# Distance table made on GpSimd from index patterns, first transfers reordered, 64-row products padded to 128 rows

## Chip, cores and metric

The kernel runs on one core of a Trainium2 chip. The metric is the device time of one execution in microseconds (us). Engines are named as the profile names them: PE (matrix products; PEld is its weight load), DVE (vector), ACT (scalar), POOL (GpSimd), and SP, whose queue starts nearly all transfers (SPq).

## The reference

Attention over 2 batches x 8 heads, 768 tokens, head size 64, followed by a low-rank token mixing with an FFN, and by a Fourier mixing with a normalisation and a second FFN. Cut to what matters:

```python
scores = q @ k.T / 8                               # per head
rel = pos[:, None] - pos[None, :]
is_global = pos[None, :] < n_global                # 8
is_local = (rel >= 0) & (rel < n_local)            # 96
dist = where(is_global & ~is_local, n_local, abs(rel))
scores = where(is_global | is_local, scores - slope[h] * dist, -1e9)
x = softmax(scores) @ v                            # -> (2, 768, 512)
u = x + (x.T @ U @ V).T                            # U (768, 32), V (32, 768)
x = u + relu(u @ w1) @ w2                          # w1 (512, 2048)
u = x + real(fft(fft(x, axis=1), axis=2))
x = u + relu(norm(u) @ w1b) @ w2b
```

All inputs are float32.

## The kernel before, in words

The program is written with a tile framework: `setup` is traced first, then `arm`, inside a branch on a flag that the device computes from the two window sizes (L70 to L72, L853). Python generators (`attn`, `lr`, `ffn`, `fft`, `norm`) yield after small steps; `arm` and `drive` interleave them. From this trace the framework's planner chooses each engine's fixed order: what is traced earlier has priority, but an instruction whose inputs are ready in the planner's own clock may be put ahead of an earlier one that still waits. Every engine, and the SP queue, then works strictly in its order. Nothing inside the branch is mixed with what is outside it.

**Start.** `setup` makes a 128 x 128 identity on POOL (a memset and one affine select, listed as masks.py), and starts on the SP queue: the window sizes `n` (L48), the table `rel` (L51), query and windowed keys of head pair 0 in two halves of 64 partitions each (L55), and the values of pair 0 (`v_load`, L408). `rel` (128 x 1184 float32: eight blocks of 128 columns with -4 x distance, or -4 x 2^20 where nothing is to be kept, and two key index patterns) is laid into the second value buffer `vb[1]`. `attn_setup` (L369) turns it with the window sizes into the mask-and-distance tables `dist[0]` (DVE, L375 to L381) and `dist[1]` (POOL, L382, half of the first). 16 products of the identity with itself (`warm`, L80) stand on PE before the branch, 10 behind it, and two after each of the first six steps of attention.

**Attention.** `attn` (L413) works on 8 head pairs c, each in three units j. A unit's steps: s1 (scores L448 and L451 on PE with 64 rows for each head, then L456 on DVE adds the table), s2 (exponential on ACT, L468), s3 (transposes on PE, L479, copied out by ACT L481 or DVE L483), s5 (weights times values, L499). s1 of unit 0 of pair c starts the loads of query and keys of pair c+1 (`qk_load`, L398 and L399); s5 of unit 2 starts the values of pair c+2. Pair 1's values go to `vb[1]`, so `v_load(1)` waits until `rel` has been read.

**Low rank.** `lr_load` (L276) loads U and V (four copies of V, L283); `lr_setup` and `lr_setup2` decode them (they come as 8-byte words; L163 on ACT, L165, L167, L169 on DVE) and split them into a high and a low float32r part: `vh` (128 rows, L311) and `vl` (64 rows, L312, on POOL). `lr` (L339) then adds, for each of 6 token tiles of a batch, two products into one bank: L352 (`vh`, 128 rows) and L353 (`vl`, 64 rows, with the first 64 rows of R).

**FFN.** `ffn` (L185) runs 96 chunks: 12 products L202, then 12 products L224, all 128 x 128 weights times 512 columns in float32r (high times high, high times low, low times high). The weights of a chunk are loaded, split by ACT (L178) and POOL (L181), and in layer 1's first pass also decoded and written back.

**Fourier mixing.** `fft` (L613, once per batch) is four groups of products beside the FFN. Each accumulation ends in one product with 64 rows, which carries the one odd row of a fold: L674 (`alt` with `em`, twice per batch), L684 (the same for one odd column; its 64 weight columns are one column repeated by `spread`, as are those of the nine L682 before it), L709 (`pr` with `sgn`, four times per batch; the fourth time with a single weight column). `fft_open` loads the constant tables on POOL's queue (L604, L608).

## Time and profile before

| | us |
|---|---|
| median of 3 runs | 728.35 |
| lowest, highest | 726.04, 732.85 |
| the profiled execution | 723.43 |
| its span, first to last instruction | 721.4 |

PE was busy for 700.0 us of the span (97%), DVE for 347.2, ACT for 294.9, POOL for 299.9; the mean granted TensorE clock was 0.996 of full speed. Times below are us from the start of the span. A busy PE is not PE at its peak: products overlap, so what a product costs is read from the start of one to the start of the next.

### The profile page before, as it was taken

Reading aid. Unit: us, or ns where it says so; the run is one execution under the profiler, and the core shown is the slowest. Engines: PE = TensorE matmul, PEld = TensorE weight load, DVE = VectorE, ACT = ScalarE, POOL = GpSimd, SP = SyncE. Lnnn points to the kernel's source line nnn. Section 1 sums busy time; section 2 is a strip of 40 time slices with the busy share of each in tenths; the row PEclk is TensorE's granted clock in tenths of the full one; section 3 lists DMA queues with packets and bytes.
Section 4 is the critical chain, followed back from the end, with each engine's and each line's share of the span. In section 5 each row is a group of like instructions: output and inputs, shape, how many; then the busy total and the mean of one; then the engine's idle time right before and its main releaser. Section 6 shows DMA issues by size and latency. Waiting matters only on the chain.

```text
span 721.4 us, 9681 instructions
## 1 busy us (share of the span) xinstructions
PE 700.0 (97%) x3584; PEld 561.7 (78%) x3584; DVE 347.2 (48%) x703; ACT 294.9 (41%) x551; POOL 299.9 (42%) x256
## 2 busy tenths in 40 slices
PE   8899999989899999999999999999999999999996
PEld 7666667767678888888788878888888888888885
DVE  3898887544652744348545769113733111211112
ACT  3877755644433434344343334322333333233230
POOL 1211202316646444556424564433554445445441
PEclk9999999999999999999999999999999999999999
DMA  8785648454658467775754442212124222242211
GB/s 274 245 322 190 223 165 254 141 174 135 216 171 255 154 228 254 247 259 178 261 176 146 146 175 89 87 59 88 58 88 159 100 93 88 99 164 87 91 56 64
DMA packets 34393, 116.54 MB, mean 162 GB/s; under 512 B 4128, under 2 KB 4384, under 8 KB 32032
## 3 DMA queue, kind: packets, MB, share of 16 engines
q1 hardware_dynamic: 33024, 112.24, 46.2%
q0 software_dynamic: 1312, 3.59, 1.6%
q8 instruction: 30, 0.49, 0.3%
q14 instruction: 27, 0.22, 0.1%
HBM read 95.88 MB, written 19.92 MB: 161 GB/s over the span
## 4 chain that ended last, share of the span: by engine, by line
PE 72%; DMA 8%; DVE 6%; POOL 5%; issue 5%; ACT 3%; SPq 0%; ACTq 0%; DVEq 0%; POOLq 0%
PE ps_acc L224 29%; PE ps_h L202 29%; DMA wr<-wl 6%; POOL wo L181 5%; PE ps_sd L499 3%; PE ps_h L479 2%; PE ps_acc L448 2%; DMA lrt<-U 1%; DVE w L169 1%; PE ps_sd L267 1%; ACT wh L178 1%; DMA w<-wscr 1%; DVE xl L334 1%; ACT wr L163 1%; PE ps_sd L448 1%
## 5 line engine op out<-in xcount | busy, mean ns | idle before, releaser
L181 POOL TENSOR_TENSOR wo<-w,wh 128x512 fp32r<-128x512 f32 x192 | 256.0, 1354 | 306.3 <-ACT wh L178 304.7
L202 PE MATMUL ps_h<-uT,wh 128*128 128x512 f32 x768 | 240.8, 394 | 0.0
L202 PEld LDWEIGHTS ps_h<-uT,wh 128*128 128x128 f32 x768 | 141.3, 188 | 30.0 <-issue 2.8
L178 ACT CAST wh<-w 128x1024 fp32r<-128x1024 f32 x96 | 100.9, 1051 | 153.5 <-PE ps_acc L224 137.3
L210 DVE SCALAR_TENSOR_TENSOR gl<-ps_h,gh 128x512 fp32r<-128x512 f32 x96 | 65.9, 687 | 188.7 <-ACT gh L209 188.6
L224 PE MATMUL ps_acc<-wh,gh 128*128 128x512 f32 x384 | 152.9, 398 | 0.0
L224 PE MATMUL ps_acc<-wh,gl 128*128 128x512 f32 x384 | 150.3, 391 | 0.8 <-DVE gl L210 0.8
L202 PE MATMUL ps_h<-uT,wo 128*128 128x512 f32 x384 | 150.1, 391 | 0.0
L224 PE MATMUL ps_acc<-wo,gh 128*128 128x512 f32 x384 | 149.7, 390 | 0.0
L209 ACT ACTIVATE gh<-ps_h 128x512 fp32r<-128x512 f32 x96 | 57.2, 596 | 123.3 <-PE ps_h L202 123.0
L224 PEld LDWEIGHTS ps_acc<-wh,gl 128*128 128x128 f32 x384 | 72.1, 188 | 17.3 <-DVE gl L210 1.9
L224 PEld LDWEIGHTS ps_acc<-wh,gh 128*128 128x128 f32 x384 | 72.1, 188 | 16.5 <-issue 2.0
L202 PEld LDWEIGHTS ps_h<-uT,wo 128*128 128x128 f32 x384 | 72.3, 188 | 15.7 <-issue 0.2
L224 PEld LDWEIGHTS ps_acc<-wo,gh 128*128 128x128 f32 x384 | 72.2, 188 | 13.8
L163 ACT ACTIVATE wr<-wr 128x1024 f32<-128x1024 f32 x32 | 37.4, 1168 | 62.8 <-DMA wr<-wl 58.9
L468 ACT ACTIVATE T<-T,m 128x256 f32<-128x256 f32 (+1 forms) x96 | 47.7, 498 | 32.4 <-DVE m L456 31.2
L165 DVE TENSOR_SCALAR wr<-wr 128x1024 int32<-128x1024 int32 x32 | 24.8, 780 | 41.0 <-DMA wr<-wl 40.9
L169 DVE SCALAR_TENSOR_TENSOR wd<-wr 128x1024 int32<-128x1024 int32 x16 | 19.6, 1224 | 48.0 <-POOL wo L181 42.9
L167 DVE SCALAR_TENSOR_TENSOR wr<-wr 128x1024 int32<-128x1024 int32 x32 | 40.4, 1264 | 4.3 <-ACT wr L163 4.1
L499 PE MATMUL ps_sd<-pt,vb 128*64 128x128 f32 x384 | 34.8, 288 | 3.4 <-ACT pt L481 3.3
L499 PEld LDWEIGHTS ps_sd<-pt,vb 128*64 128x64 f32 x384 | 26.0, 139 | 11.1 <-issue 5.3
L456 DVE CUSTOM_DVE_ANT_0 T<-ps_acc,dist 128x256 f32<-128x256 f32 (+1 forms) x76 | 28.0, 419 | 5.6 <-PE ps_acc L451 3.6
(160 smaller groups left out, 606.0 us busy)
## 6 DMA issues: line engine op xcount, KB each, us to landing
w<-wscr SPq DMA_DIRECT2D x80, 512.0 KB, 3.3
wr<-wl SPq DMA_DIRECT2D x17, 1024.0 KB, 6.0
wr<-wl SPq DMA_DIRECT2D x60, 256.0 KB, 4.5
wscr<-w SPq DMA_DIRECT2D x16, 512.0 KB, 6.7
wscr<-wd SPq DMA_DIRECT2D x16, 512.0 KB, 2.9
vb<-vw SPq DMA_DIRECT2D x8, 768.0 KB, 5.4
out<-qkt SPq DMA_DIRECT2D x12, 256.0 KB, 3.3
k<-qkg SPq DMA_DIRECT2D x4, 704.0 KB, 8.5
```

The lines of the kernel that those rows point to most:

```text
L163: nc.scalar.activation(hi.bitcast(F32), hi.bitcast(F32), AF.Copy, scale=2.0 ** -112)
L167: nc.vector.scalar_tensor_tensor(lo, hi, 3, lo, ALU.logical_shift_left, ALU.bitwise_or)
L169: nc.vector.scalar_tensor_tensor(out.bitcast(I32), hi, -2147483648, lo, ALU.bitwise_and, ALU.bitwise_or)
L178: nc.scalar.copy(hi, raw)
L181: nc.gpsimd.tensor_tensor(lo[:, h], raw[:, h], hi[:, h].bitcast(F32), ALU.subtract)
L202: nc.tensor.matmul(hp, lhsT=w[:, s], rhs=u[:, dd, :], start=n == 0, stop=n == 11)
L209: nc.scalar.activation(gh, hp, AF.Relu)
L210: nc.vector.scalar_tensor_tensor(gl, hp, 0.0, gh.bitcast(F32), ALU.max, ALU.subtract)
L224: nc.tensor.matmul(acc[t], lhsT=g[:, s], rhs=w[:, D:2 * D], start=pf == 0 and m == 0, stop=pf == NF - 1 and m == 2)
L456: nc.vector.tensor_tensor_reduce(out=T[z][:, s], in0=sp[z][:, s], in1=self.dist[z][:, dcol[t]:dcol[t] + width[t]], op0=ALU.add, op1=ALU.mi ...
L468: nc.scalar.activation(T[z][:, s], T[z][:, s], AF.Exp, bias=m[z][:, i:i + 1], scale=-1.0, accum_out=st["s", c, z][:, j, i:i + 1])
L499: nc.tensor.matmul(pv[y * HD:(y + 1) * HD, z * P:(z + 1) * P], lhsT=v[:, vc, d], rhs=pt[z][:, o:o + P], start=i == 0, stop=i == n - 1)
```

## The change

The load of `rel` is gone; `rel_make` writes the same 1184 columns with 15 POOL instructions (seven iotas for the blocks and keys, two affine selects, three memsets, then an iota, a select and a memset for the last 256 columns). `v_load(1)` moves from ahead of attention to behind its second step, `lr_load` from behind the sixth step to behind the twelfth; `lr_setup` still comes after 22. The 64-row operands `vl`, `alt`, `sgn`, `em` get 64 more rows of zeros (one memset each, on POOL for `vl`, else on DVE), `pr` and the two column-spread products get 128 weight columns in place of 64 or 1, so that L353, L674, L684, L709 become 128-row products and L682, L684 and the fourth L707 and L709 have 128 columns.

```diff
--- before.py
+++ after.py
@@ -48,12 +48,12 @@
         nc.sync.dma_start(ni.rearrange("p a b -> p (a b)"), self.rows(a["n"].bitcast(I32), 4))
         self.qk, self.v = {}, {}
         self.rel, self.key = self.vb[1][:, 0:WTAB], self.vb[1][:, WTAB:WTAB + P + 32]
-        nc.sync.dma_start(self.vb[1][:, 0:WTAB + P + 32], a["rel"])
         self.qk = {0: (self.qkt[:, 0:S], self.qkt[:, S:S + KW])}
         for z in range(2):
             s = slice(z * HD, (z + 1) * HD)
             nc.sync.dma_start(self.qkt[s, 0:S + KW], a["qkg"][0][s])
         self.v_load(0)
+        self.rel_make()
         ok = cp.tile([1, 4], F32, name="ok")
         nc.scalar.activation(ok[:, 3:4], self.ident[0:1, 0:1], AF.Exp)
         nf = cp.tile([P, 2, 2], F32, name="nf")
@@ -293,7 +293,8 @@
         uraw = ur.rearrange("p (t r) -> p t r", t=NT)
         self.us = pool.tile([P, NT, 4 * RK], FR, name="us")
         self.vh = pool.tile([P, S], FR, name="vh")
-        self.vl = pool.tile([2 * RK, S], FR, name="vl")
+        self.vl = pool.tile([P, S], FR, name="vl")
+        nc.gpsimd.memset(self.vl[2 * RK:P, :].bitcast(F32), 0.0)
         us = self.us
         for c in (0, 2):
             h, l = us[:, :, c * RK:(c + 1) * RK], us[:, :, (c + 1) * RK:(c + 2) * RK]
@@ -309,7 +310,7 @@
             self.decode(vraw, v64, z)
             yield
         nc.scalar.copy(self.vh, vraw)
-        nc.gpsimd.tensor_tensor(self.vl, vraw[0:2 * RK, :], self.vh[0:2 * RK, :].bitcast(F32), ALU.subtract)
+        nc.gpsimd.tensor_tensor(self.vl[0:2 * RK, :], vraw[0:2 * RK, :], self.vh[0:2 * RK, :].bitcast(F32), ALU.subtract)
         yield
 
     def w_first(self):
@@ -350,7 +351,7 @@
             s = slice(t * P, (t + 1) * P)
             hp = self.psum("m")
             nc.tensor.matmul(hp, lhsT=self.vh[:, s], rhs=R, start=True, stop=False)
-            nc.tensor.matmul(hp, lhsT=self.vl[:, s], rhs=R[0:64, :], start=False, stop=True)
+            nc.tensor.matmul(hp, lhsT=self.vl[:, s], rhs=R, start=False, stop=True)
             nc.vector.tensor_tensor(x, hp, x, ALU.add)
             yield
             if t > 0 and b * NT + t - 1 in tiles:
@@ -365,6 +366,38 @@
             self.transpose_in(layer, i, srcs[i])
             yield
 
+
+
+    def rel_make(self):
+        g = self.nc.gpsimd
+        FAR = -4.0 * (1 << 20)
+
+        def put(out, base, step, ch, blocks=None):
+            pat = [[4, P]] if blocks is None else [[step, blocks], [4, P]]
+            v = out if blocks is None else out.rearrange("p (a c) -> p a c", a=blocks)
+            g.iota(v, pat, base=base, channel_multiplier=ch, allow_small_or_imprecise_dtypes=True)
+
+        def cut(o, base, ch, blocks=1):
+            v = self.rel[:, o:o + blocks * P].rearrange("p (a c) -> p a c", a=blocks)
+            g.affine_select(out=v, in_=v, compare_op=ALU.is_ge, fill=FAR, base=base,
+                            pattern=[[0, blocks], [-1, P]], channel_multiplier=ch)
+
+        rel = self.rel
+        put(rel[:, 384:640], -512, -512, 4, 2)
+        put(rel[:, 0:256], 0, 0, -4, 2)
+        cut(384, P, -1)
+        cut(0, 0, 1, 2)
+        put(rel[:, 256:384], -512, 0, -4)
+        put(rel[:, 640:768], -4 * 511, 0, 4)
+        put(rel[0:1, 640:768], -4 * 127, 0, 0)
+        g.memset(rel[0:1, 384:640], FAR)
+        for o in (256, 512):
+            g.memset(rel[:, o:o + 32], FAR)
+        g.iota(self.key[:, 0:P], [[1, P]], base=0, channel_multiplier=0, allow_small_or_imprecise_dtypes=True)
+        g.iota(self.key[:, P:P + 32], [[1, 32]], base=0, channel_multiplier=0, allow_small_or_imprecise_dtypes=True)
+        put(rel[:, 768:1024], -4 * 127, -512, 4, 2)
+        cut(768, P - 1, -1)
+        g.memset(rel[:, 896:928], FAR)
 
     def attn_setup(self):
         nc = self.nc
@@ -604,8 +637,9 @@
                 nc.gpsimd.dma_start(t, a[f"{n}{z}"])
                 self.ct[n, z] = t
         for n, r, w in (("alt", 64, J1), ("sgn", 64, K1)):
-            t = fp.tile([r, w], FR, name=n)
-            nc.gpsimd.dma_start(t, a[n])
+            t = fp.tile([P, w], FR, name=n)
+            nc.vector.memset(t[r:P, :].bitcast(F32), 0.0)
+            nc.gpsimd.dma_start(t[0:r, :], a[n])
             self.ct[n] = t
         self.mh = fp.tile([P, 1], F32, name="mh")
         nc.vector.memset(self.mh, -0.5)
@@ -648,18 +682,19 @@
             fold(P, E, False, ee[0][:, i, :], ee[1][:, i, :], i)
             fold(P, O, True, oo[0][:, i, :], oo[1][:, i, :], i)
             yield
-        em = fp.tile([64, K1], FR, tag="em", bufs=1, name=f"em{b}")
-        fold(64, xm, False, em, None, 0)
+        em = fp.tile([P, K1], FR, tag="em", bufs=1, name=f"em{b}")
+        nc.vector.memset(em[64:P, :].bitcast(F32), 0.0)
+        fold(64, xm, False, em[0:64, :], None, 0)
         yield
         c1, s1, c2, s2 = ([ct[n, 0], ct[n, 1]] for n in ("c1", "s1", "c2", "s2"))
         pt = fp.tile([P, 2, 2, J1], FR, tag="fpt", bufs=1, name=f"fpt{b}")
         qt = fp.tile([P, 2, 2, 384], FR, tag="fqt", bufs=1, name=f"fqt{b}")
         pt, qt = [pt[:, z] for z in range(2)], [qt[:, z] for z in range(2)]
-        pr = fp.tile([64, J1], FR, tag="fpr", bufs=1, name=f"fpr{b}")
+        pr = fp.tile([P, J1], FR, tag="fpr", bufs=1, name=f"fpr{b}")
         PS = ((0, 0), (0, 1), (1, 0))
 
         def spread(col):
-            return bass.AP(col.tensor, col.offset, [list(col.ap[0]), [0, 64]])
+            return bass.AP(col.tensor, col.offset, [list(col.ap[0]), [0, P]])
 
         for dd in range(2):
             cs = slice(dd * P, dd * P + P)
@@ -675,7 +710,7 @@
             nc.scalar.copy(pt[0][:, dd, :], pp)
             nc.vector.tensor_tensor(pt[1][:, dd, :], pp, pt[0][:, dd, :].bitcast(F32), ALU.subtract)
             yield
-        pp = self.psum("m")[0:64, 0:J1]
+        pp = self.psum("m")[:, 0:J1]
         n = 0
         for i in range(3):
             for x, y in PS:
@@ -702,11 +737,12 @@
 
         def pcos(out, js):
             n = 0
+            at = (lambda v: spread(v[:, 384:385])) if js is None else (lambda v: v[:, js])
             for dd in range(2):
                 for x, y in PS:
-                    nc.tensor.matmul(out, lhsT=pt[x][:, dd, js], rhs=c2[y][:, dd, :], start=n == 0, stop=False)
+                    nc.tensor.matmul(out, lhsT=at(pt[x][:, dd, :]), rhs=c2[y][:, dd, :], start=n == 0, stop=False)
                     n += 1
-            nc.tensor.matmul(out, lhsT=pr[:, js], rhs=ct["sgn"], start=False, stop=True)
+            nc.tensor.matmul(out, lhsT=at(pr), rhs=ct["sgn"], start=False, stop=True)
 
         for i in range(3):
             js = slice(i * P, (i + 1) * P)
@@ -730,7 +766,7 @@
                 nc.vector.tensor_tensor(X[:, 511:256:-1], X[:, 511:256:-1], hi_[:, 1:256], ALU.add)
             yield
         pc = self.psum("m")
-        pcos(pc[0:1, 0:K1], slice(384, 385))
+        pcos(pc[:, 0:K1], None)
         X = Bp[0]
         nc.vector.tensor_tensor(X[0:1, 0:257], pc[0:1, 0:257], xm[0:1, 0:257], ALU.add)
         nc.vector.tensor_tensor(X[0:1, 511:256:-1], pc[0:1, 1:256], xm[0:1, 511:256:-1], ALU.add)
@@ -786,14 +822,16 @@
         pg.at = pool
         pg.side_mode = False
         if fast:
-            pg.v_load(1)
             att = pg.attn(pool)
             pg.warm(10)
-            for _ in range(6):
+            for z in range(6):
                 step(att, 1)
+                if z == 1:
+                    pg.v_load(1)
                 pg.warm(2)
+            step(att, 6)
             pg.lr_load()
-            step(att, 16)
+            step(att, 10)
             for _ in pg.lr_setup(pool):
                 step(att, 2)
             pg.w_load(0)
```

## Rows read from the trace of the kernel before

**Rows 1.** Stretches: length, busy PE, PEld, DVE, ACT, POOL; clock, DMA share, GB/s.
```profile
86.00:99.00 13.00, 12.85 (x89) 8.50 (x84) 11.42 (x30) 7.82 (x23) 0.00 (x0) 1.00 0.74 251
194.00:520.00 326.00, 325.25 (x1483) 264.14 (x1484) 169.41 (x271) 117.29 (x163) 156.88 (x131) 1.00 0.51 172
```
**Rows 2.** Waits of PE from 194 to 520: total, times, longest.
```profile
PE ps_acc L224 <- DVE gl L210: 0.8, 2, 0.5
```
**Rows 3.** Chain that ended last, pieces: start, length, what.
```profile
10.38 8.95 DMA lrt<-U
...
92.54 0.43 PE ps_acc L353
...
217.71 2.72 PE ps_h L202 x12
```
**Rows 4.** Timeline of PE around one low-rank pair: start, length, what.
```profile
204.44 0.40 PE L352 MATMUL ps_sd<-R,vh 128*128 128x512 f32 x1
204.76 0.49 PE L353 MATMUL ps_sd<-R,vl 64*128 64x512 f32 x1
205.19 0.73 PE L202 MATMUL ps_h<-uT,wh 128*128 128x512 f32 x2
205.75 0.40 PE L202 MATMUL ps_h<-uT,wo 128*128 128x512 f32 x1
```
**Rows 5.** Groups by form, 64-row products: count, busy, mean ns.
```profile
L353 PE MATMUL ps_sd<-R,vl 64*128 64x512 f32 x6 | 3.0, 494 | 0.0
L709 PE MATMUL ps_sd<-sgn,fpr 64*128 64x258 f32 x6 | 2.3, 381 | 0.0
L674 PE MATMUL ps_sd<-alt,em 64*128 64x386 f32 x4 | 1.8, 443 | 0.0
L709 PE MATMUL ps_sd<-sgn,fpr 64*1 64x258 f32 x2 | 0.5, 272 | 0.0
```
**Rows 6.** Timeline of PE before and after the wide spread products.
```profile
359.02 0.39 PE L224 MATMUL ps_acc<-wh,gl 128*128 128x512 f32 x1
359.24 1.75 PE L682 MATMUL ps_sd<-c,ee 128*64 128x386 f32 x9
```
**Rows 7.** Timeline of DVE at the start.
```profile
5.91 0.30 DVE L375 TENSOR_SCALAR vb<-vb,nv 128x160 f32<-128x160 f32 x1 [0.97 <-DMA vb<-rel]
8.12 0.83 DVE L381 SCALAR_TENSOR_TENSOR dist<-vb,nv,dist 128x128 f32<-128x128 f32 x4
11.91 0.29 DVE L456 CUSTOM_DVE_ANT_0 T<-ps_acc,dist 128x128 f32<-128x128 f32 x1 [2.85 <-PE ps_acc L451]
19.35 0.26 DVE L165 TENSOR_SCALAR lrt<-lrt 128x192 int32<-128x192 int32 x1 [3.64 <-DMA lrt<-U]
```
**Rows 8.** Timeline of PE at the start.
```profile
10.91 0.70 PE L448 MATMUL ps_acc<-qkt 64*128 64x128 f32 x5 [1.18 <-DMA qkt<-qkg]
20.35 0.85 PE L479 MATMUL ps_h<-ident,T 128*128 128x128 f32 x6 [2.03 <-DVE pt L483]
```
**Rows 9.** Timeline of the SP queue: start, length, transfer.
```profile
17.75 0.35 SPq L398 DMA_DIRECT2D qkt<-qkg  x1
18.62 0.42 SPq L129 DMA_DIRECT2D wr<-wl  x1
29.18 0.33 SPq L408 DMA_DIRECT2D vb<-vw  x1
```
**Rows 10.** DMA issues: count, KB each, us from issue to landing.
```profile
vb<-rel SPq DMA_DIRECT2D x1, 592.0 KB, 4.7
```
**Rows 11.** Stretches of the start, columns as in rows 1.
```profile
5.00:9.00 4.00, 4.00 (x36) 4.00 (x36) 3.05 (x9) 0.00 (x0) 0.00 (x0) 1.00 1.06 243
11.00:17.00 6.00, 6.00 (x50) 5.18 (x52) 2.93 (x16) 4.40 (x17) 0.83 (x1) 1.00 1.03 411
```
**Rows 12.** Timeline of POOL at the start.
```profile
1.01 0.29 POOL masks.py:199 TENSOR_SCALAR_AFFINE_SELECT ident<-ident 128x128 f32<-128x128 f32 x1
```
**Rows 13.** The page's costliest group, on POOL: busy, mean ns | idle before, releaser.
```profile
L181 POOL TENSOR_TENSOR wo<-w,wh 128x512 fp32r<-128x512 f32 x192 | 256.0, 1354 | 306.3 <-ACT wh L178 304.7
```

## Prediction

> **What bounds the kernel now.** I read the busy times by stretch first, then the waits of PE, then the chain that ended last, and the timelines of the start last. From 194 to 520 PE is busy for 325.25 of 326 us while no other engine reaches 170 [rows 1], and in all that time its longest kind of wait, for DVE, adds up to 0.8 us [rows 2]; behind 520 nothing changes in the code. So there a product that goes, or gets cheaper, shortens the run one for one. Before 194 the stages differ. At the very start PE and DVE wait for transfers: DVE stands 3.64 us in front of the decoding of U, which lands at 19.35, though that decoding has no hurry; it only stands early in DVE's order, and the copy of the first transposes behind it holds PE for 2.03 us [rows 7, 8]. The chain confirms it: its earliest long piece is U's transfer, 10.38 to 19.33 [rows 3]. Between, around 86 to 99, PE is busy nearly throughout, but its products there are short, and DVE with 11.42 of 13 us is near its limit too [rows 1].
>
> **The padded products.** There are 22 products with 64 rows: twelve L353, four L674, two L684, six L709 with 128 columns and two with one (the rows show six of the L353; the others and the L684 follow from the code) [rows 5]. Their cost isn't their own length alone. The normal step is 2.72 us for 12 products of 512 columns, 0.227 us each [rows 3]. Around one pair the starts are 204.44 (L352), 204.76 (L353), 205.19 and, two products on, 205.75 [rows 4]: four products of 512 columns in 1.31 us in place of 0.91, so 0.40 us too much. It stands in three places: about 0.09 before the 64-row product may start, 0.20 on itself, 0.11 on what follows. With 128 rows, nothing but the normal step should stay. Outside the first six L353 there are 16 products of full width (6 + 4 + 6) at 0.40, 6.4 us; the narrow L709 is 109 ns shorter than the wide one [rows 5], so I price the two of it and the two L684 at 0.29, 1.2 us. All 20 lie between 194 and 520: 7.5 us (7.6 rounded down, since 258 columns may lose a little less). From below I would only believe the modelled lengths, which show some 0.1 us too much for each (494 ns [rows 5] against 0.40 us of a normal one [rows 4]): 2.0 us. From above 20 x 0.40, 8.0 us.
>
> The first six L353 lie among products of attention that themselves use 64 rows, so that the change of form moves rather than goes. The chain does run through them, 0.43 us each [rows 3]. Fully saved they are worth 6 x 0.40 = 2.4, hidden 0; I take 1.0, because DVE is nearly full there.
>
> The Trainium skill, "TensorEngine Tiling (Array Packing)", section Key Properties, says that a change of tiling mode drains TensorE. It lists column widths among the modes; by that the change from 128 to 64 weight columns and back in the nine L682 would cost as well, and widening them would give back, by an estimate, 0.2 us twice over in each batch, making the padding 8.3. The trace agrees for rows and differs for columns: L224 at 359.02 is followed by the first L682 at 359.24, the normal step [rows 6]. The rows decide: nothing for columns.
>
> **The first transfers.** `rel` is 592 KB, 0.606 MB. It takes 4.7 us from issue to landing [rows 10], most of it latency. The transfer engines are full from 5 us on, at 243 GB/s while the 64-partition halves of the query load and at 411 GB/s later [rows 11]; 0.606 MB is 1.5 us at the one rate and 2.5 at the other. Everything queued behind it comes that much earlier; I take 2.0 us. U now stands behind pair 1's query, keys and values, as before, so it lands at about 17.3. Is the wait on U still last? The first scores could start 1.18 us earlier, where PE now waits for the second half of the query [rows 8], so the first DVE step comes at 10.7 and DVE is free for U at 14.5, still ahead of 17.3. What follows on PE is then 2.0 us earlier. If U's decoding moves back in DVE's order, the wait goes altogether, and the limit is PE's own: 2.03 and 1.18 of idle time, 3.2 us. Behind the start the shift should pass to the end: pair 1's data are 2 us earlier too, later loads are released by PE.
>
> **The table on POOL.** The first twelve instructions of `rel_make` make the 768 columns and the keys, 1,760 columns written in all; the last three are beside DVE's first part. No iota is in the trace. The nearest row is an affine select of 128 columns, 0.29 us, 2.3 ns a column [rows 12]; by it, 4.0 us, ready at 1.3 + 4.0 = 5.3, earlier than the 5.91 at which DVE now starts on `rel` [rows 7]. From above, the dearest kind of POOL row, 1.354 us [rows 13], twelve times is 16.2 us, ready at 17.5. DVE then needs 3.1 us (5.91 to 8.95), and from the first score step to the copy behind U 3.8 (11.91 to 19.35 less the wait of 3.64) [rows 7]. The copy starts at 19.5 now; with the table ready at 12.6 it would start there without any wait for U. So the table costs nothing up to 10.4 (where U at 17.3 is still last), and at 17.5 it is 4.9 us late against now. I take 0, by the nearest row.
>
> **What is added elsewhere.** `v_load(1)` now has two loads ahead of it and still waits until the table is read, at about 8.5; `lr_load` stands behind it on the SP queue and waits with it, but what is ahead in the transfer queue keeps that busy until 12 or so: nothing. The memset of `vl` (64 x 768) goes to POOL, which waits 306 us in total for ACT [rows 13]; the memsets of `alt`, `sgn` and twice `em`, about 0.4 us each by an estimate from the 0.30 us of 160 columns [rows 7], go to DVE, busy for 169 of 326 us [rows 1]. Where DVE is late for PE now (0.8 us [rows 2]) they may add a little: 0.3 us. Without that cover all of it would cost 1.6.
>
> **The sum.** 7.5 + 1.0 + 2.0 - 0.3 = 10.2 us. The profiled execution took 723.43 us (span 721.4 and 2.0 around it), so it would take 713.2. That execution is 4.9 us below the median of the runs shown, 728.35; taken from that, 718.2 us.
>
> **Rivals.** (a) *U falls behind pair 2.* `lr_load` is now traced behind the step that asks for pair 2's query and keys. If the planner keeps that order, those wait for PE (17.75 now [rows 9], 16.5 then), and U, with 1.1 MB ahead of it, lands at about 21.5; with its decoding where it stands, the start loses 2.2 us in place of gaining 2.0: gain 6.0, 722.4 us. Against it: a weight load that is traced later already goes ahead of the values that wait for PE (18.62 before 29.18 [rows 9]), so what is ready isn't kept back.
> (b) *The rows don't matter.* The extra step belongs to something else, such as a bank or the operands' place: padding gains nothing, 2.0 - 0.3, 726.7 us. Against it: the step is the same for four lines with different operands. The Trainium skill speaks for it: "TensorE: Matmul & The Clock Gate", section Why this matters for your kernels, has a product with few rows take as long as one with 128. The trace disagrees, 0.43 us against 0.23 [rows 4].
> (c) *Slower: the table comes late.* Each iota may cost far more than a select, or each change between the two kinds may stop POOL. The start loses from a table ready at 12.6, and the whole change loses once it loses 8.2 there, with the table ready at 20.8: twelve instructions in 19.5 us, 1.6 us each, more than the dearest row. At 22 us of POOL the table is ready at 23.3, the copy starts at 30.2, 10.7 us late, and the time is 728.35 + 10.7 - 8.2 = 730.9. For it: no row shows an iota. Against it: the select follows its memset without a gap [rows 12]. The Trainium skill, "GPSIMD Engine Reference", section Instruction dispatch, tells of about 6 us, unseen in the profile, for the first call of a newly loaded kernel; three such loads would give just these 22 us, one would still hide behind U. No run here shows one.
>
> **How the numbers follow.** Forecast 0.70, (a) 0.16, (b) 0.07, (c) 0.07. The likeliest case alone runs from 8.0 + 2.4 + 3.2 = 13.6 gained to 7.5 + 1.5 - 0.5 = 8.5, so 714.7 to 719.9. The runs of before lie 2.3 below and 4.5 above their median; with that and (a) the range is 712 to 726. A change of 1% (7.3 us) is about what a measurement tells from none. Faster by more: 0.63 of the forecast's 0.70, 0.06 of (a): 0.69. Slower by more: part of (c), with a table later still: 0.03. The rest, 0.28, is within 1%.
>
> **What would show it.** Starts around L353, L674 and L709 at the normal step (0.23, 0.17, 0.12 us), their sum some 7 to 8 us; U's landing at 17 to 17.5 and the transposes behind it at about 18.3 in place of 20.35; `rel_make` finished before 6; and the point where PE becomes saturated 3 us earlier. The prediction is wrong if iotas take over a microsecond each, if U lands after 19.3, or if the steps of the padded products stay at 0.3 us or more; also if a different planned order in attention or the first FFN block, which nothing in the trace of before can show, gives back what the start gained.

## The result, and the profile after

The changed kernel takes 718.77 us (median of 6 runs, 715.34 to 720.31) against 727.25 us (6 runs, 724.39 to 732.85): ratio 0.9889, 95% interval 0.9856 to 0.9923. Forecast were 718.2 us and a range of 712 to 726. The total came as forecast; its make-up did not, and most of what follows is about that.

One caution for every comparison of traces below. The profiled execution of before (723.43 us) lies 3.8 us under the median of its runs and below all six of them; that of the changed kernel (720.31) is the slowest of its six. So the two traces differ by 3.1 us only, where the medians differ by 8.5. Their spans hide another microsecond: the last chunk starts 3.9 us earlier than before, but from the start of PE's last product to the end it took 6.17 us in the trace of before and 7.19 in that of after. I therefore follow the starts of the FFN's chunks.

The page's busy times (share of the span, instructions), against 700.0, 347.2, 294.9 and 299.9 us before:

```profile
PE 692.2 (96%) x3584; PEld 563.0 (78%) x3584; DVE 346.9 (48%) x707; ACT 294.3 (41%) x551; POOL 301.3 (42%) x272
```

**The start.** The timeline of the changed kernel on POOL, SP, DVE and PE (SPq is SP's issue of a transfer; brackets give the engine's idle time before the row, and what ended it); it answers to [rows 7 to 9, 12].

```profile
0.98 0.35 POOL L378 IOTA vb<- 128x256 f32 x1
1.30 0.28 POOL masks.py:199 TENSOR_SCALAR_AFFINE_SELECT ident<-ident 128x128 f32<-128x128 f32 x1
...
4.16 0.29 POOL L382 TENSOR_SCALAR_AFFINE_SELECT vb<-vb 128x128 f32<-128x128 f32 x1
4.39 0.12 POOL L400 MEMSET vb<- 128x32 f32 x1
...
4.74 0.60 DVE L410 TENSOR_SCALAR dist<-vb,nv 128x768 f32<-128x768 f32 x1
...
7.97 0.33 SPq L441 DMA_DIRECT2D vb<-vw  x1
8.40 0.38 SPq L280 DMA_DIRECT2D lrt<-U  x1
...
11.13 0.29 DVE L489 CUSTOM_DVE_ANT_0 T<-ps_acc,dist 128x128 f32<-128x128 f32 x1 [2.67 <-PE ps_acc L484]
...
16.14 0.26 DVE L165 TENSOR_SCALAR lrt<-lrt 128x192 int32<-128x192 int32 x1 [1.40 <-DMA lrt<-U]
...
17.20 1.04 PE L512 MATMUL ps_h<-ident,T 128*128 128x128 f32 x8
```

An iota of 256 columns takes 0.34 us and the whole of `rel_make` is over at 4.51; DVE begins on the table at 4.74 without a wait, directly behind its own set-up. U lands at 16.14 instead of 19.35, DVE waits 1.40 us for it instead of 3.64, and the second transposes start at 17.20 instead of 20.35. U's transfer starts at 8.40, ahead of pair 2's query at 16.79, so rival (a) of the prediction did not come.

**The padded products.** The groups by form and one low-rank pair in the timeline, changed kernel, in answer to [rows 4, 5].

```profile
L354 PE MATMUL ps_sd<-R,vl 128*128 128x512 f32 x6 | 2.4, 393 | 0.0
L745 PE MATMUL ps_sd<-sgn,fpr 128*128 128x258 f32 x8 | 2.2, 281 | 0.0
L709 PE MATMUL ps_sd<-alt,em 128*128 128x386 f32 x4 | 1.4, 338 | 0.0
```
```profile
199.85 0.40 PE L202 MATMUL ps_h<-uT,wo 128*128 128x512 f32 x1
200.09 0.40 PE L353 MATMUL ps_sd<-R,vh 128*128 128x512 f32 x1
200.32 0.39 PE L354 MATMUL ps_sd<-R,vl 128*128 128x512 f32 x1
200.55 0.62 PE L202 MATMUL ps_h<-uT,wh 128*128 128x512 f32 x2
```

From start to start it is now 0.23 us before, on and behind the padded product, where [rows 4] showed 0.32 and 0.43, and 0.56 for the next two together (0.46 is normal). The Fourier products' steps are normal too in this trace: 0.18 us around L709 and L719, 0.12 around L745.

**And yet PE waits.** PE's waits of the changed kernel from 194 to 520 (line, releaser: us in total, times, longest) and the two stretches of [rows 1], with two short ones. Columns of the second fence: length, busy PE, PEld, DVE, ACT, POOL, granted clock, DMA share, GB/s.

```profile
PE ps_acc L224 <- DVE gl L210: 2.4, 3, 1.0
PE ps_h L202 <- POOL wo L181: 1.6, 1, 1.6
PE ps_acc L224 <- ACT gh L209: 1.2, 1, 1.2
PE ps_sd L353 <- DVE xall L355: 0.5, 1, 0.5
```
```profile
86.00:99.00 13.00, 12.69 (x77) 8.44 (x77) 11.54 (x29) 7.57 (x21) 0.83 (x1) 1.00 0.79 257
194.00:520.00 326.00, 320.10 (x1482) 266.15 (x1482) 171.27 (x276) 117.77 (x164) 156.90 (x133) 0.99 0.50 168
...
213.00:218.00 5.00, 3.08 (x13) 1.95 (x12) 3.49 (x5) 3.08 (x4) 0.91 (x1) 1.00 1.02 376
218.00:222.00 4.00, 4.00 (x13) 3.10 (x12) 0.23 (x1) 0.24 (x1) 4.00 (x7) 0.57 0.42 140
```

The PE that stood still for 0.75 us of these 326 now does so for 5.9. From 213 to 218 it is busy for 3.08 of 5 us, and behind these gaps the granted clock has a mean of 0.57 from 218 to 222: for a time it was at the lower of its two levels, 1.2 GHz.

**Where the time went.** First product of a chunk against the kernel before, us (negative is earlier), worked out from the traces' starts of L202; "unit 3" is the first score product of pair 1. The last column is the last chunk.

```
kernel          unit 3   c0    c10    c12    c14    c34    c36    c44    c46    c52   last
before at        22.81 104.86 194.79 211.53 222.99 333.92 347.40 405.93 418.48 453.34
changed          -3.18  -7.27  -4.63  -5.56  -1.52  -1.44  -0.95  -3.29  -1.30  -1.30  -3.90
after_again      -3.16  -6.93  -5.28  -5.37  -0.99   0.27   0.75  -1.56  -0.25  -0.27  -2.87
pad_only         -0.52  -1.56  -1.06  -1.71   0.92   1.86   2.40   0.09   1.40   1.38  -1.23
start_only       -2.80  -6.11  -4.50  -3.90  -3.90  -2.96  -2.19  -2.19  -1.59  -1.62  -1.62
fft_pad_only            -6.51  -4.09  -3.54  -3.52  -3.68  -3.19  -4.88  -2.79  -2.85  -5.45
cols_narrow             -6.56  -4.52  -6.05  -3.25  -3.45  -3.16  -5.47  -3.79  -3.79  -6.39
wr16_pool               -7.54  -5.86  -7.34  -5.00  -5.18  -5.15  -7.47  -5.77  -5.80  -8.40
wr17_pool        -2.96  -7.36  -5.68  -7.42  -7.42  -6.88  -6.40  -8.71  -7.22  -7.25  -9.85
xm_dve                  -7.21  -5.38  -6.02  -3.34  -3.42  -2.94  -5.05  -3.28  -3.30  -5.90
both_supplies           -6.33  -4.11  -5.18  -5.18  -4.79  -4.31  -6.36  -5.49  -5.52  -8.12
old_loads        -2.54  -3.60  -3.50  -3.87  -1.65  -1.08  -0.61  -2.67  -0.89  -0.92  -3.52
table_x3          0.29  -3.96  -2.62  -3.82   0.22   0.97   1.44  -0.87   0.96   0.90  -1.71
u_first_w4       -3.20  -3.73  -3.21  -4.95  -0.94   0.13   0.62  -1.59   0.52   0.50  -2.10
```

In the changed kernel's line, the Fourier padding shows at c36 to c44 (2.34 us) and from c52 on (2.60). In *start_only*, which has no padding, both stretches gain nothing. Three places give time back: c0 to c10 (2.6), c12 to c14 (4.0), and c44 to c46 (2.0). The experiments ask what these are.

### The profile page after: what moved, and what is told of

It reads as the page before. It is cut to its first block, busy times and chain, and to the rows that moved or that the text cites. A ratio compares the mean times of both kernels' runs of the same rounds, so it can differ in the third digit from the quotient of the medians.

```text
span 718.5 us, 9700 instructions
## 1 busy us (share of the span) xinstructions
PE 692.2 (96%) x3584; PEld 563.0 (78%) x3584; DVE 346.9 (48%) x707; ACT 294.3 (41%) x551; POOL 301.3 (42%) x272
## 4 chain that ended last, share of the span: by engine, by line
PE 73%; DVE 7%; DMA 7%; POOL 5%; issue 4%; ACT 3%; SPq 0%; ACTq 0%; POOLq 0%; DVEq 0%
PE ps_acc L224 30%; PE ps_h L202 29%; DMA wr<-wl 7%; POOL wo L181 4%; PE ps_sd L532 2%; PE ps_acc L481 2%; PE wu L80 2%; PE ps_h L512 1%; ACT T L501 1%; PE ps_sd L267 1%; ACT wh L178 1%; PE ps_sd L729 1%; DVE w L169 1%; POOL xl L335 1%; PE ps_sd L705 1%
## 5 line engine op out<-in xcount | busy, mean ns | idle before, releaser
L181 POOL TENSOR_TENSOR wo<-w,wh 128x512 fp32r<-128x512 f32 x192 | 254.2, 1345 | 313.9 <-ACT wh L178 312.3
L202 PE MATMUL ps_h<-uT,wh 128*128 128x512 f32 x768 | 241.2, 395 | 0.0
L202 PEld LDWEIGHTS ps_h<-uT,wh 128*128 128x128 f32 x768 | 142.3, 189 | 29.6 <-issue 2.0
L224 PE MATMUL ps_acc<-wh,gl 128*128 128x512 f32 x384 | 151.1, 394 | 2.4 <-DVE gl L210 2.4
L224 PE MATMUL ps_acc<-wh,gh 128*128 128x512 f32 x384 | 152.2, 396 | 1.2 <-ACT gh L209 1.2
L202 PE MATMUL ps_h<-uT,wo 128*128 128x512 f32 x384 | 150.8, 393 | 1.6 <-POOL wo L181 1.6
L224 PE MATMUL ps_acc<-wo,gh 128*128 128x512 f32 x384 | 150.5, 392 | 0.0
L224 PEld LDWEIGHTS ps_acc<-wh,gl 128*128 128x128 f32 x384 | 72.5, 189 | 19.1 <-DVE gl L210 3.6
L202 PEld LDWEIGHTS ps_h<-uT,wo 128*128 128x128 f32 x384 | 72.4, 189 | 17.5 <-POOL wo L181 2.0
L224 PEld LDWEIGHTS ps_acc<-wh,gh 128*128 128x128 f32 x384 | 72.5, 189 | 16.4 <-ACT gh L209 1.7
L224 PEld LDWEIGHTS ps_acc<-wo,gh 128*128 128x128 f32 x384 | 72.5, 189 | 13.8
L532 PE MATMUL ps_sd<-pt,vb 128*64 128x128 f32 x384 | 32.5, 282 | 4.2 <-ACT pt L514 4.1
```

The lines of the kernel that those rows point to most:

```text
L181: nc.gpsimd.tensor_tensor(lo[:, h], raw[:, h], hi[:, h].bitcast(F32), ALU.subtract)
L202: nc.tensor.matmul(hp, lhsT=w[:, s], rhs=u[:, dd, :], start=n == 0, stop=n == 11)
L224: nc.tensor.matmul(acc[t], lhsT=g[:, s], rhs=w[:, D:2 * D], start=pf == 0 and m == 0, stop=pf == NF - 1 and m == 2)
L532: nc.tensor.matmul(pv[y * HD:(y + 1) * HD, z * P:(z + 1) * P], lhsT=v[:, vc, d], rhs=pt[z][:, o:o + P], start=i == 0, stop=i == n - 1)
```

## The experiments

**Each half alone, and the whole again.** *pad_only* has the padding alone, the table and the loads as before; *start_only* has the table and the moved loads alone. The main lines of *start_only*'s edit against before:

```diff
-        nc.sync.dma_start(self.vb[1][:, 0:WTAB + P + 32], a["rel"])
+        self.rel_make()
...
-            pg.v_load(1)
...
+                if z == 1:
+                    pg.v_load(1)
```

*after_again* is the changed kernel unaltered, for a second profile; *cols_narrow* is the changed kernel with the weights of L717 and L719 narrowed to 64 columns again, and of the last pass of L743 and L745 to one (the 64 rows of `pr` that are then not written are zeroed on DVE, not shown):

```diff
-            return bass.AP(col.tensor, col.offset, [list(col.ap[0]), [0, P]])
+            return bass.AP(col.tensor, col.offset, [list(col.ap[0]), [0, 64]])
```

> The kernel before with the padding alone: rel is loaded again, v_load(1) and lr_load stand where they stood. Theory (the padding carries most of the gain, product by product): the steps around the 20 padded products between 194 and 520 fall by 0.3 to 0.4 us each, 7.5 us in all, U lands at 19.3 as before, and the time falls by 7 to 8.5 us, a ratio of 0.988 to 0.991. Rival 1 (the start carries it, the padded steps are given back at other waits): a fall of under 4 us, ratio above 0.9945. Rival 2 (a planned order that only by chance is better): the starts of the first FFN chunk come 3 us or more earlier although nothing of the start has changed.

> The kernel before with the table on POOL and the moved loads, 64-row products as before. Theory: U lands 3.2 us earlier as in the changed kernel, PE's transposes of unit 1 start at 17.2 in place of 20.35, and 2 to 3.5 us of it reach the end: ratio 0.995 to 0.9975. Rival 1 (the start carries the gain): 5 us or more, ratio below 0.993. Rival 2 (the start's gain is given back to the weight loads between 130 and 220): under 1 us, ratio above 0.9985, with first FFN products that start 3 us or more earlier.

> The changed kernel, unaltered, for a second profile. The first one showed PE losing about 4 us between 214 and 222 (waits on ACT and DVE behind a weight load that landed late, and 3.4 us at half the granted clock). If that belongs to the order of the program, it stands here again in the same chunk (13 of the FFN), and the clock falls there again; if it belongs to that one execution, the shift of the FFN's starts against the kernel before stays between 4 and 7 us over chunks 12 to 16, and the span is 3 to 5 us below 718.5.

> The changed kernel with its 128 rows, but the spread products with 64 weight columns and the last cosine product with one, as before. If only the rows matter: each step around L682, L684 and the fourth L707 and L709 stays at 0.17 to 0.18 (386 columns) and 0.12 us (258 columns), and the time is that of the changed kernel within 1 us. If a change of column width drains PE as well: about 0.1 us before and 0.1 to 0.2 us behind each of the four groups, 0.8 to 1.2 us in all.

Measured, against 725.64 us for before: *pad_only* 724.51, ratio 0.9978 (0.9952 to 1.0004); *start_only* 722.74, 0.9956 (0.9932 to 0.9981); *after_again* 719.35, 0.9911 (0.9877 to 0.9945); *cols_narrow* 718.10, 0.9901 (0.9875 to 0.9927).

*start_only* came in its range. *pad_only* missed by far: each step fell as argued, but the time fell by 1.1 us, as its rival 1 had it, and its interval reaches past 1. Its line in the table says where: 2.6 us lost from c12 to c14, 1.3 from c44 to c46. *after_again* loses at the same places, so the losses belong to the program and not to one execution. *cols_narrow* cannot be told from the changed kernel. Its timeline on PE has the narrow products in normal steps, 0.23 us from L224 to the first of them (355.38, 355.61) and 0.18 each:

```profile
355.38 0.39 PE L224 MATMUL ps_acc<-wh,gl 128*128 128x512 f32 x1
355.61 1.75 PE L718 MATMUL ps_sd<-c,ee 128*64 128x386 f32 x9
357.19 0.34 PE L720 MATMUL ps_sd<-alt,em 128*64 128x386 f32 x1
357.37 0.39 PE L224 MATMUL ps_acc<-wh,gh 128*128 128x512 f32 x1
```

The last cosine product with one weight column has its normal 0.12 us too. So it is the rows alone, as the prediction had it against the Trainium skill ("TensorEngine Tiling (Array Packing)", section Key Properties): that page has a change of tiling mode drain the engine, and counts column widths among the modes.

**What stands at c12 to c14.** The changed kernel there, on SP, POOL, ACT and PE:

```profile
203.42 2.20 SPq L129 DMA_DIRECT2D wr<-wl  x4
...
204.71 1.33 POOL L637 DMA_DIRECT2D c<-c  x2 [3.01 <-PE ps_sd L354]
...
209.48 1.10 POOL L637 DMA_DIRECT2D s<-s  x2
210.56 0.55 POOL L637 DMA_DIRECT2D c<-c  x1
...
214.42 1.17 ACT L163 ACTIVATE wr<-wr 128x1024 f32<-128x1024 f32 x1 [5.76 <-DMA wr<-wl]
215.49 0.58 ACT L209 ACTIVATE gh<-ps_h 128x512 fp32r<-128x512 f32 x1
...
216.12 0.50 PE L224 MATMUL ps_acc<-wh,gh 128*128 128x512 f32 x1 [1.24 <-ACT gh L209]
217.54 0.50 PE L224 MATMUL ps_acc<-wh,gl 128*128 128x512 f32 x1 [0.68 <-DVE gl L210]
```

A weight load in four parts is issued at 203.42; from 204.71 the Fourier constants come on POOL's queue, released by the last low-rank product (L354). The load is there only at 214.4. ACT stands 5.76 us in front of its decoding, and `gh`, for which PE waits, stands behind that in ACT's order (it is chunk 12's, which PE uses behind chunk 13's L202). Two edits test it: take the competing transfers away from the load, or leave the low-rank products as long as they were, so that PE asks later and releases the constants later. At first I moved the wrong load, the one ahead of it (k is NF for *wr16_pool*, NF + 1 for *wr17_pool*; the four parts are NF + 1). *fft_pad_only* leaves the low-rank products at 64 rows.

```diff
-        self.nc.sync.dma_start(self.wraw[k].rearrange("p n t -> p (n t)")[:, s],
+        (self.nc.gpsimd if k == NF + 1 else self.nc.sync).dma_start(self.wraw[k].rearrange("p n t -> p (n t)")[:, s],
```
```diff
-        self.vl = pool.tile([P, S], FR, name="vl")
-        nc.gpsimd.memset(self.vl[2 * RK:P, :].bitcast(F32), 0.0)
+        self.vl = pool.tile([2 * RK, S], FR, name="vl")
...
-            nc.tensor.matmul(hp, lhsT=self.vl[:, s], rhs=R, start=False, stop=True)
+            nc.tensor.matmul(hp, lhsT=self.vl[:, s], rhs=R[0:64, :], start=False, stop=True)
```

> The changed kernel, but the load of layer 1's first weights (wr16, 1 MB) goes on POOL's queue, directly ahead of the Fourier constants (3.6 MB), instead of on SP's queue beside them. Theory (supply): in the changed kernel this load takes about 11 us (issued 203.4 to 205.2, landing 214.4) because it shares the transfer engines with the constants; ACT's decode of it stands ahead of chunk 13's gh, so PE waits 1.4 + 0.85 us and falls to half clock for 3.4 us. With the load first in one queue it lands within 6 us of its issue, ACT does not wait, PE has no wait over 0.5 us between 200 and 225 and no half clock there; chunk 14 starts 4.0 to 5.5 us earlier than in the kernel before (changed kernel: 1.5 and 1.0), and the time is 2.5 to 4 us below the changed kernel: 715 to 717. Rival (the two queues are not what makes it late; the weights' own chain does): chunk 14 stays 1 to 2 us earlier than before, time 718 to 720.

> The changed kernel with the twelve low-rank products L354 left at 64 rows; the Fourier ones stay padded. Theory (supply): what padding saves in the second six (2.4 us) only brings PE earlier to a wait for weights at chunk 13, so giving it back costs less than it: chunk 14 starts no more than 0.5 us later than in the changed kernel, perhaps earlier if PE then misses the wait and the half clock, and the time is within 1.5 us of the changed kernel, 717.5 to 720.5. Rival (each padded product pays one for one, as predicted): 2.4 us for the second six and 1.0 for the first, time 3.4 us above the changed kernel, 721.5 to 723.

> The changed kernel, but layer 1's second weights (wr17, 1 MB in four parts, the load that was issued 203.4 to 205.2 and landed at 214.4) go on POOL's queue directly ahead of the Fourier constants. The run wr16_pool had moved the load before it, and there the four parts still took 11 us. Theory (supply): alone at the head of the one queue the four parts land within 7 us of the first issue; the decode on ACT no longer holds gh of chunk 13, so both PE waits at 213 to 217 (1.4 and 0.85 us) and the half clock behind them are gone; chunk 14 starts 4.5 to 5.5 us earlier than in the kernel before and the time is 714.5 to 717. Rival (PE is ahead of something else there too, for instance gl or the weights read back): other waits of 1.5 us or more in all stand between 205 and 222, chunk 14 is 1 to 3 us earlier than before, time 717.5 to 720.

*wr16_pool*: 717.04 us, ratio 0.985 (0.9796 to 0.9904). Its time is at the upper end of the range (717), but not for the reason given: the four parts still landed at 212.5, 10.8 us after their issue, and PE still waited for `gh`; what is missing is half clock behind it. *fft_pad_only*: 718.60, 0.9858 (0.9800 to 0.9917), the same as the changed kernel, and c14 comes 2.0 us earlier than there although six products are 0.40 us dearer each. *wr17_pool*: 715.35 (714.62 to 716.83), 0.9840 (0.9805 to 0.9876). Its timeline on POOL and ACT:

```profile
201.46 2.41 POOL L129 DMA_DIRECT2D wr<-wl  x4 [1.57 <-DVE w L169]
203.85 0.56 POOL L637 DMA_DIRECT2D c<-c  x1
...
208.24 1.18 ACT L163 ACTIVATE wr<-wr 128x1024 f32<-128x1024 f32 x1 [2.69 <-DMA wr<-wl]
209.28 0.61 ACT L269 CAST uT<-ps_sd 128x512 fp32r<-128x512 f32 x1
209.75 0.64 ACT L209 ACTIVATE gh<-ps_h 128x512 fp32r<-128x512 f32 x1
```
```profile
213.00:218.00 5.00, 5.00 (x24) 4.14 (x23) 0.69 (x1) 1.65 (x2) 4.73 (x7) 1.00 1.08 367
218.00:222.00 4.00, 4.00 (x19) 3.30 (x19) 0.69 (x1) 1.35 (x2) 1.49 (x2) 1.00 1.16 326
```

The load is there 6.8 us after its issue, PE has no wait and full clock (second fence, the stretches as above), and from c12 to c14 nothing is lost. The time is in its range; c14 comes 7.42 us earlier than before, where 4.5 to 5.5 were expected. The shift at the last chunk is 9.85 us instead of 3.90, of which 1.9 us were there by c12, ahead of this load. (The planner also put the decoding one copy earlier in ACT's order.) So the stall is shown to be the late load; the edit took away the constants beside it and the SP queue together.

What made the load late can be read by setting all the traces side by side. The columns, worked out from the starts, count us from the issue of the load's first part: to the first constant's issue, to ACT's decoding, to `gh` of chunk 12 being done, and to the moment PE could use it (the last L202 of chunk 13 and one normal step); the last is what is lost from c12 to c14. The nine kernels of the second line are the changed one, *after_again*, *pad_only*, *cols_narrow*, *wr16_pool*, *xm_dve*, *old_loads*, *table_x3* and *u_first_w4*.

```
kernel                             constants   decoding      gh done     PE asks    lost
before, start_only, fft_pad_only   1.88-1.89   8.0-8.8       9.6-10.4    12.1       0.0
nine with low-rank padding         1.25-1.32   10.7-11.3     12.4-13.0   11.2-11.3  2.2-4.4
wr17_pool, both_supplies           2.38-2.39   6.8           8.9-9.0     11.4-11.5  0.0
```

So it is not a matter of how far PE is ahead of before: *start_only*, 3.9 us ahead at c12, loses nothing, and *pad_only*, 1.7 us ahead, loses 2.6. The last low-rank product releases the constants. Padded, it ends sooner, and they start 0.6 us nearer to the load, beside its last two parts instead of behind all four; the decoding then begins 2 to 3 us later. PE itself asks only 0.8 us sooner, which alone would have cost nothing, with `gh` there at 9.6 to 10.4. No run moves the constants alone. Five of the nine keep a granted clock of 1.00 behind the gap and lose 2.2 to 2.8 us; the four whose clock fell (0.57 to 0.82 from 218 to 222: the changed kernel, *after_again*, *table_x3*, *u_first_w4*) lose 4.0 to 4.4.

**What the start is worth.** *old_loads* is the changed kernel with the loads started where before starts them; *table_x3* makes the table three times over; *u_first_w4* starts U and V ahead of the values of pair 1 and has 4 warm-ups instead of 10 behind the branch:

```diff
-        self.rel_make()
+        for _ in range(3):
+            self.rel_make()
```
```diff
-            pg.warm(10)
+            pg.warm(4)
...
                 if z == 1:
+                    pg.lr_load()
                     pg.v_load(1)
...
-            step(att, 6)
-            pg.lr_load()
-            step(att, 10)
+            step(att, 16)
```

> The changed kernel with the values of pair 1 and the low-rank loads started where the kernel before started them (values of pair 1 first, then query and keys of pair 1, then U and V). Theory (the table off the queue is the whole gain; the transfer engines are busy until about 10 us anyway): U lands within 0.5 us of the changed kernel's 16.1, the first transposes start at 17.2 to 17.8, time within 1 us of the changed kernel. Rival (the moved loads matter, since the values of pair 1 wait for the table to be read and hold query, keys and U behind them on SP): U lands at 17.5 or later, the transposes at 18.5 or later, time 1.5 to 2.5 us above the changed kernel.

> The changed kernel with the table made three times over on POOL, so that it is ready about 7.1 us later (first part at 11 instead of 3.8). Theory: the table then is the last thing at the start. DVE's table chain begins at about 11.9 instead of 4.74 and ends at about 15.1; the values of pair 1 wait for it on the SP queue and hold U behind them until about 15.5, so U lands at 18.5 to 20 and the transposes start at 20 to 21.5 instead of 17.2: 3 to 4.5 us lost, time 721.5 to 723.5. Rival (the prediction's slack: with the table ready up to 10.4 nothing is lost, and after that one for one): the transposes start at 17.8 to 18.2, 0.6 to 1 us lost.

> The changed kernel with U and V started ahead of the values of pair 1, and 4 in place of 10 warm-up products behind the branch. At the start: U lands at 14 to 15 instead of 16.1, and the first transposes start at 15 to 16 instead of 17.2. Theory (supply): the first FFN block goes at the pace of its weights, so an earlier start is used up there: the 1.2 to 2 us won are 0.5 or less by chunk 14, and the time is within 0.8 us of the changed kernel. Rival (a shift at the start passes to the end, as predicted): the time is 1.2 to 2 us below the changed kernel.

*old_loads*: 722.10 (719.05 to 728.67), ratio 0.9913 (0.9867 to 0.9959). U lands at 16.81 and unit 3 is 2.54 us earlier than before: the moved loads give only 0.6 of the start's 3.2, the table 2.5. Another 3.0 us that the changed kernel wins between units 8 and 11 are missing (below). Neither expectation came as written: U is 0.67 us later than in the changed kernel, and the median 3.3 us above 718.77. The intervals of the two ratios overlap, though, and at the last chunk *old_loads* is 3.52 us ahead of before, the changed kernel 3.90.

*table_x3*: 721.80, 0.9934 (0.9899 to 0.9969). Its timeline on SP and DVE:

```profile
9.71 0.62 DVE L411 TENSOR_SCALAR dist<-vb,nv 128x768 f32<-128x768 f32 x1 [4.71 <-POOL vb L396]
...
13.50 0.33 SPq L442 DMA_DIRECT2D vb<-vw  x1
13.93 0.78 SPq L281 DMA_DIRECT2D lrt<-U  x1
...
19.63 0.26 DVE L166 TENSOR_SCALAR lrt<-lrt 128x192 int32<-128x192 int32 x1 [2.82 <-DMA lrt<-U]
```

A table that is ready at 9.7 costs 3.5 us at unit 3, not nothing. The values of pair 1 wait for the table to be read, U stands behind them on SP, and from 13 to 14 the transfer engines move nothing (share 0.00). The slack that the prediction gave the table (up to 10.4) was not there.

*u_first_w4*: 719.85 (719.54 to 722.48), 0.9894 (0.9849 to 0.9940), so no better than the changed kernel. U lands at 14.33, in range, but the second transposes start at 16.71 (15 to 16 expected) and unit 3 at 19.61, against 19.63. From 13.83 to 17.34 PE's row shows no wait there, so its own order is the limit, and U holds up nobody. Since nothing was won at unit 3, this says nothing on whether a win would pass to the end.

**POOL at c44 to c46.** *xm_dve* zeroes `xm` on DVE instead of POOL; *both_supplies* joins that to *wr17_pool*.

```diff
-        nc.gpsimd.memset(xm, 0.0)
+        nc.vector.memset(xm, 0.0)
```

> The changed kernel with the zeroing of xm (64x512, at the start of each Fourier mixing) on DVE instead of POOL; in the changed kernel POOL stands 3.20 us for it at 406 and needs 1.07 us, with two chunks' wo behind it, and PE then waits 1.75 us for wo at 408.75. Theory (POOL's order is what gives back the padding's gain between chunks 44 and 46): that wait falls to 0.3 us or less, the shift against the kernel before shrinks by under 1 us from chunk 44 to 46 (changed kernel: from 3.29 to 1.30), and the time is 1 to 2 us below the changed kernel. Rival (the normalization's two small POOL steps alone make wo late): the wait stays above 1 us and the time within 0.7 us of the changed kernel.

> The edits of wr17_pool and xm_dve together. Theory (the padding's lost gain sits at these two places): their gains add, chunk 14 starts 4.5 to 5.5 us earlier than in the kernel before, chunk 62 8 to 10 us earlier, time 713 to 716, under both the kernel before and the changed kernel. Rival: what is won at the first place is lost at the second or behind it, time 716.5 to 719.

*xm_dve*: 718.31 (717.31 to 720.31), 0.9879 (0.9832 to 0.9926): PE's wait for `wo` is still 1.34 us and 1.8 us are lost from c44 to c46, so my cause is wrong, as the rival had it. POOL's timeline in that kernel:

```profile
404.79 0.57 POOL L783 TENSOR_SCALAR mv<-mv 128x1 f32<-128x1 f32 x1 [3.32 <-DVE mv L782]
405.45 1.99 POOL L784 TENSOR_TENSOR mv<-mv,mh 128x1 f32<-128x1 f32 x1
407.41 2.50 POOL L181 TENSOR_TENSOR wo<-w,wh 128x512 fp32r<-128x512 f32 x2
```

POOL stands just as long for the normalization's `mv`, which DVE makes behind the Fourier additions, with `wo` behind it. That is read from the rows and was not tried. *both_supplies*: 716.66 (713.76 to 718.92), 0.9853 (0.9814 to 0.9892): no loss from c12 to c14, 0.9 us instead of 2.0 at c44 to c46, but 1.0 us less at c0 and 1.6 less at c10; no better than *wr17_pool*, and in the range of its rival. *wr17_pool* is the fastest version found, by its median. Timed side by side, its slowest run (716.83) was below the fastest of *xm_dve* (717.31); against the changed kernel's own runs the two intervals still touch.

## Why the prediction was right, and where it was not

**The padded products' price was right.** Every step fell to normal. The 14 Fourier products were priced at 5.2 us (10 x 0.40 + 4 x 0.29) and gave 2.34 + 2.60 = 4.9; *pad_only* has 2.31 + 2.61 there. For the first six low-rank products 1.0 us was counted, and *pad_only* gains 1.05 from unit 16 to c0. (There are 26 products with 64 rows, not 22; the sum took 20 + 6 and is not touched by it.) Rival (b), that the rows don't matter, is out. The Trainium skill ("TensorE: Matmul & The Clock Gate", section Why this matters for your kernels) has a single product with few rows take as long as one with 128; a 64-row product between 128-row ones took 0.43 us here against 0.23.

**The step that failed: "there a product that goes, or gets cheaper, shortens the run one for one".** I read PE's saturation from 194 on as a property of PE. But PE's products also release transfers and other engines' work, and the 0.8 us of waits held for that order of events alone. Of 7.5 us counted there, the changed kernel's trace keeps none (4.63 us ahead at c10, 3.90 at the end). 4.0 us went at c12 to c14, where the low-rank padding brought the constants beside a weight load; *fft_pad_only*, without it, loses nothing there. 2.0 went at 408, on POOL's `wo`, and half a microsecond at c34 to c36, on DVE's `gl`. These two are not the padding's alone: *start_only* loses 0.6 and 0.8 there. It has none of the small memsets that I had allowed 0.3 us for, so they don't explain the second. With the load first in one queue (*wr17_pool*) the stretch keeps 4.2 us (5.68 to 9.85).

**The start was under-sized.** Forecast were 2.0 us and measured 3.2, its upper bound, though for another reason: DVE still waits for U, but U lands at 16.1 and not at 17.3. By *old_loads* the table alone is worth 2.5 us, the upper of the two prices that the prediction made from its bytes; the moved loads, which the sum had at nothing, gave the other 0.6. (Iotas took 1.3 ns a column instead of the 2.3 priced; DVE, busy with its own set-up until then, had no wait for the table.) The prediction had nothing lost with a table up to 10.4, and a loss against before from 12.6 on: *table_x3*, ready at 9.7, loses 3.5 us against the changed kernel and starts unit 3 0.3 us later than before. The step left out is that pair 1's values wait for the table to be read, with U behind them on SP.

**A gain that I had not seen.** From unit 8 to unit 11 the lead over before grew from 4.02 to 6.98 us. In before, POOL's second pair of `wo` (L181) runs beside DVE's `xl` subtractions; both engines read two tensors in SBUF. PE waits 1.5 us for `xl` there, and 0.2 in the changed kernel. Before and after, DVE and POOL:

```profile
51.12 0.41 DVE L334 TENSOR_TENSOR xl<-xall,xh 128x256 fp32r<-128x256 f32 x1
54.02 2.83 DVE L334 TENSOR_TENSOR xl<-xall,xh 128x256 fp32r<-128x256 f32 x2
...
53.89 2.69 POOL L181 TENSOR_TENSOR wo<-w,wh 128x512 fp32r<-128x512 f32 x2 [3.91 <-ACT wh L178]
```
```profile
49.42 0.41 DVE L335 TENSOR_TENSOR xl<-xall,xh 128x256 fp32r<-128x256 f32 x1
50.09 0.41 DVE L335 TENSOR_TENSOR xl<-xall,xh 128x256 fp32r<-128x256 f32 x1
51.46 0.41 DVE L335 TENSOR_TENSOR xl<-xall,xh 128x256 fp32r<-128x256 f32 x1
...
46.10 2.51 POOL L181 TENSOR_TENSOR wo<-w,wh 128x512 fp32r<-128x512 f32 x2 [7.89 <-ACT wh L178]
59.79 0.84 POOL L434 TENSOR_SCALAR q<-q 128x768 f32<-128x768 f32 x1 [11.18 <-DMA q<-qkg]
```

The planner put that second pair later (60.71) once the loads were traced elsewhere: in *pad_only*, *old_loads* and *u_first_w4*, with POOL's old order, the gain is absent, in *start_only* and *table_x3* it is there. So it goes with the order, which moving the loads changed by accident; that the overlap of the two engines is the cause was not tried by itself.

**It was mostly given back between c0 and c10.** The kernels that are 6 us or more ahead at c0 have 4.1 to 5.9 left at c10 and lost 1.6 to 2.6; *old_loads*, 3.60 ahead, lost 0.1. It may be the order again and not the lead: *table_x3*, with POOL's new order, is 3.96 ahead and loses 1.3, while *pad_only* and *u_first_w4*, with the old one, lose 0.5 each. Between 100 and 225 PE of the changed kernel waits 4.1 us for ACT's copies of the transposes and 4.2 us for POOL's `xl`, that of before 3.3 and 3.8; 1.4 us for DVE's `xall` stand in the changed kernel alone. Which of them sets the pace I haven't tried.

**Why the total still came out.** By the traces the changed kernel won 3.9 us at the last chunk, where the sum said 10.2. The medians say 8.5, because the profiled run of before was faster than all six of its runs and that of after the slowest of its own. In the next round *after_again* was 6.3 us below before's median, and the halves 1.1 and 2.9. Where the other runs of before lose their time, no trace shows. So the close hit is partly luck: too little allowed for the front (3.0 us, of which 7.3 came at c0 and 4.6 were left at c10), too much for what comes behind 194, and a sum made on one execution and set on the median.

## What to carry to other kernels

Near-zero waits of a busy engine hold for the order of events in that trace. Before counting savings one for one, ask what each shortened piece of work releases (a transfer, a split, a decode), what that will run into, and which load is ready only just in time. When bulk constants come into the same stretch as a load that is needed at once, put them behind it in one queue, as *wr17_pool* did. A table made on chip still has a due time: the first thing on the queue that waits for its buffer, since all that stands behind it on that queue waits too.

## What the runs showed that I had not expected

The narrow forms: a change from 128 to 64 rows and back costs 0.40 us for one product of 512 columns, from 128 to 64 weight columns nothing (0.23 us from start to start). An `xl` of 0.41 us took 1.4 us on average beside POOL's two-input subtraction; POOL's 128x1 power took 1.99 us instead of 0.57 in one place, in *xm_dve* and *both_supplies*. An iota of 128 x 256 took 0.34 us, and the first one of the program was no slower (0.35); of the 6 us that the Trainium skill ("GPSIMD Engine Reference", section Instruction dispatch) tells of for the first call of a newly loaded kernel, unseen in the profile, POOL's timeline has no gap: iota at 0.98, select at 1.30, the whole table at 4.51.
